# Precedence for VectorE's additions of the projection, and other half steps for its products

## The chip, the cores and the metric

The kernel runs on one core of a Trainium2 chip. The metric is the device time of one execution in microseconds (us). Five engines work side by side, each with an instruction queue of its own: TensorE (PE in the profile) does matrix products and writes them into PSUM; VectorE (DVE) and ScalarE (ACT) read PSUM and do elementwise work; GpSimd (POOL) and SyncE (SP) here only issue transfers between the memories. They wait for each other by semaphores.

## The reference

Sliding-window attention with a distance bias, and after it a gated feed-forward block on 4608 tokens:

```python
q, k, v: (8, 8, 576, 64)                     # batch, heads, sequence, head width
rel = pos[:, None] - pos[None, :]
mask = (rel >= 0) & (rel < 128)
scores = np.where(mask, q @ k.T / sqrt(64) - slope[h] * abs(rel), -1e9)
attn = softmax(scores) @ v                   # (8, 8, 576, 64)
x = attn.transpose(0, 2, 1, 3).reshape(4608, 512)

g = x @ w_gate                               # 512 x 1536
silu = g * (1.0 / (1.0 + np.exp(-g)))
val = x @ w_val                              # 512 x 1536
out = (silu * val) @ w_out                   # 1536 x 512, float32 out
```

The last product, with `w_out`, is called the projection here.

## The kernel before

The 4608 tokens are cut into nine blocks of 512. For each block, the gate and value products fill 12 pairs of PSUM tiles (`pg`, `pv`), one pair for each 128 columns of `w_gate` and `w_val`. Each tile is a group of four matmuls, and is one half step. From a pair, ScalarE makes `tt = tanh(pg / 2)`, VectorE `uu = (tt + 1) * pg` and then `hT = uu * pv`. The factor 0.5 that is missing is applied when the projection leaves PSUM.

```python
    def gate(n, m, pg, c0=0, c1=512):
        ...
        nc.scalar.activation(tt, pg[:, c0:c1], AF.Tanh, scale=0.5)
        nc.vector.scalar_tensor_tensor(out=uu, in0=tt, scalar=one if (n, m) == PIN else 1.0,
                                       in1=pg[:, c0:c1], op0=ALU.add, op1=ALU.mult)

    def val(n, m, pv, c0=0, c1=512):
        ...
        nc.vector.tensor_mul(hT[n][:, m, c0:c1], acted[(n, m)][1][:, c0:c1], pv[:, c0:c1])

    def gate_val(n, m):
        c0 = 384 if (n, m) in acted else 0
        gate(n, m, wide(n, m, "g"), c0)
        yield
        val(n, m, wide(n, m, "v"), c0)
        yield
```

The projection of a block runs during the next block's half steps. It uses a scheme after Strassen and Winograd, with seven products in place of eight, twice for a block (`t` is 0 and 1: two pieces of 128 rows of either row half). Sums of parts of `hT` (`S1` to `S4`, lines 485 to 488, on VectorE) and of `w_out` (`T1` to `T4`) are made ahead. Each product is six matmuls with 256 columns. `X` and `Y` are the two halves of one PSUM buffer, `po`, of which there is one; `p2` is a buffer of the pool that the attention also uses, with four of them. Between two `yield`s lies one step, counted 0 to 6 in what follows:

```python
    def strassen(n, t):
        ...
            po = ps_f.tile([P, 2, HC], FP32, name="po", tag="po", bufs=1)
            X, Y = po[:, 0, :], po[:, 1, :]
            p2 = (ps_f.tile([P, HC], FP32, name="p2", tag="gv") if seeded
                  else ps_a.tile([P, HC], FP32, name="p2", tag="a"))
        ...
        def half_plus(dst, a, b):
            nc.vector.scalar_tensor_tensor(out=dst, in0=a, scalar=factor, in1=b,
                                           op0=ALU.mult, op1=ALU.add)

        product(X, A11, B11, True)              # step 0
        ...
            nc.scalar.mul(p1s, X, factor)
        yield
        product(p2, A12, B21, not seeded)       # step 1
        ...
            half_plus(top[:, 0:HC], p2, p1s)
        ...
        yield
        product(X, S2, T2)                      # step 2
        nc.scalar.mul(u2s, X, factor)
        yield
        product(Y, S1, T1, end)                 # step 3
        ...
            nc.scalar.mul(p5s, Y, factor)
        yield
        product(X, S3, T3)                      # step 4
        half_plus(low[:, HC:DM], X, p5s)
        ...
        yield
        product(Y, S4, B22)                     # step 5
        half_plus(top[:, HC:DM], Y, u2s)
        store(n, t, top, HC if end and t else 0, DM, end)
        yield
        product(X, A22, T4)                     # step 6
        ...
            nc.scalar.mul(low[:, 0:HC], X, factor)
        store(n, t + 2, low, 0, HC if end and t else DM, end)
        yield
```

(The comments with the steps' numbers were added here.) In the loop, a block `n` from 2 to 5 has 24 half steps, `2 * m + half`, and the 14 steps of the projection of block `n - 1` follow those half steps that are in `AT`. After each step the loop lets go of one or two of the sums that wait in `later`:

```python
    AT = {1, 3, 4, 6, 8, 9, 11, 12, 14, 16, 17, 19, 20, 22}

    def ffn():
        for n in range(NBLK):
            if n > 1:
                parts = chain(strassen(n - 1, 0), strassen(n - 1, 1))
            ...
            if n == SEVEN_FROM:                 # 6
                break
            for m in range(NMB):                # 12
                for half, _ in enumerate(gate_val(n, m)):
                    yield 1.0
                    if n > 1 and 2 * m + half in AT:
                        next(parts)
                        yield 0.75
                    if n > 1:
                        for _ in range(1 + (len(later) > 3)):
                            if later:
                                later.pop(0)()
```

The attention is made piece by piece between these steps: scores (`ps`, `psc`) into four PSUM buffers, their exponentials on ScalarE (`ex`, `exc`), the mask on VectorE, the weighted values (`av`), whose division on VectorE gives `rec` and `x`, and the transposed `x` (`px`, `xT`). The blocks 6 to 8 make their gate and value products by seven products as well.

From step 60 on, the order of TensorE alone is that of the program. The other engines' queues are filled by a scheduler, by priority, as it expects the work to become ready; at run time each queue is then worked off in that order:

```python
            if step >= FIXED_FROM and fixed is not None:
                fixed.enter_context(tc.manual_schedule(engines=ENGINES["pe"]))
```

Of the kernel before, what the change touches and what calls it, by code (L numbers as in the profile page):

```python
# [13 lines left out]
ALU = mybir.AluOpType  # L14
# [17 lines left out]
SEVEN_FROM = 6  # L32
# [19 lines left out]
def kernel(  # L52
# [10 lines left out]
    nc = tc.nc  # L63
# [377 lines left out]
    def store(n, j, osb, c0=0, c1=512, two=False):  # L441
        for i, (p0, p1, r0) in enumerate(rows_of(n, j)):
            (nc.scalar if two and i else nc.sync).dma_start(out[r0:r0 + p1 - p0, c0:c1],
                                                            osb[p0:p1, c0:c1])
# [59 lines left out]
    def strassen(n, t):  # L504

        h = hT[n]
        A11, A12 = h[:, 0:HM, 0:256], h[:, HM:NMB, 0:256]
        S1, A22 = h[:, 0:HM, 256:512], h[:, HM:NMB, 256:512]
        S2, S3, S4 = hsum[n]
        cols = slice(t * P, (t + 1) * P)  # L510
        end = n == NBLK - 1
        seeded = SEVEN_FROM <= n + 1 < NBLK
        factor = 1.0 if n >= SEVEN_FROM else 0.5
        if end:
            X, Y = (ps_a.tile([P, HC], FP32, name="po", tag="a", bufs=4) for _ in range(2))
            p2 = ps_f.tile([P, HC], FP32, name="p2", tag="gv")
        else:
# [4 lines that stand above are left out]
        top, low = (opool.tile([P, DM], FP32, name="osb", tag="osb") for _ in range(2))  # L522
        if end and t:
            spare = [opool.tile([P, DM], FP32, name="osb", tag="osb") for _ in range(2)]
            p1s, p5s, u2s = spare[0][:, 0:HC], spare[0][:, HC:DM], spare[1][:, 0:HC]
        else:
            p1s, p5s, u2s = (supool.tile([P, HC], FP32, name=i, tag=i, bufs=1)
                             for i in ("p1s", "p5s", "u2s"))

        def product(dst, a, b, start=False):  # L530
            for m in range(HM):
                nc.tensor.matmul(dst, a[:, m, cols], b[:, m, :], start=(start and m == 0),  # L532
                                 stop=(m == HM - 1), skip_group_check=True)

        def half_plus(dst, a, b):
            nc.vector.scalar_tensor_tensor(out=dst, in0=a, scalar=factor, in1=b,
                                           op0=ALU.mult, op1=ALU.add)

        product(X, A11, B11, True)
        if seeded:  # L540
            nc.scalar.copy(p2, X)
        else:
            nc.scalar.mul(p1s, X, factor)
        yield
        product(p2, A12, B21, not seeded)
        if seeded:
            nc.vector.tensor_scalar_mul(top[:, 0:HC], p2, factor)
        else:
            half_plus(top[:, 0:HC], p2, p1s)
        if end and t:  # L550
            store(n, t, top, 0, HC)
        yield
        product(X, S2, T2)
        nc.scalar.mul(u2s, X, factor)
        yield
        product(Y, S1, T1, end)
        if end and t:
            nc.vector.tensor_scalar_mul(p5s, Y, factor)
        else:
            nc.scalar.mul(p5s, Y, factor)  # L560
        yield
        product(X, S3, T3)
        half_plus(low[:, HC:DM], X, p5s)
        if end and t:
            store(n, t + 2, low, HC, DM, True)
        yield
        product(Y, S4, B22)
# [3 lines that stand above are left out]
        product(X, A22, T4)  # L571
        if end:
            nc.vector.tensor_scalar_mul(low[:, 0:HC], X, factor)
        else:
# [3 lines that stand above are left out]
# [118 lines left out]
                    of[which[0]][name](which[1])  # L696
                yield n, 7 * u + k, name, which

    AT = {1, 3, 4, 6, 8, 9, 11, 12, 14, 16, 17, 19, 20, 22}

    def ffn():

        for n in range(NBLK):
# [8 lines left out]
            for m in range(NMB):  # L712
# [4 lines that stand above are left out]
# [288 lines left out]
```

## Time and profile before

| | before |
|---|---|
| time, median of 3 (lowest, highest) | 345.17 us (344.97, 345.27) |
| span of the profiled execution | 343.0 us |
| TensorE busy | 329.1 us, 96% |
| VectorE busy | 277.5 us, 81% |
| ScalarE busy | 207.6 us, 61% |
| additions of the projection on VectorE (L536) | 42, mostly 417 ns each |

The span is one execution as the profiler saw it. L536 is line 536 of the kernel. A group is named by what it writes and reads, `po<-T,S` for a product that writes `po` from `T` and `S`. Busy matmuls overlap: a matmul of 512 columns is shown with some 379 ns, while the next one starts about 0.21 us after it. The chain that ended last is followed back from the last instruction, at each step to what released it, so its shares say which engine the end hung on. The list of waits sums, for each pair, how long an engine stood still until another released it.

### The profile page before, as it was taken

The numbers are of one execution on the slowest core, as the hardware profiler recorded it, in microseconds if no ns is written. First come the engines' busy times: TensorE is split into PE (matmuls) and PEld (weight loads), VectorE is DVE, ScalarE is ACT, GpSimd is POOL, SyncE is SP. The second block draws the span as 40 slices with busy tenths as digits, with TensorE's granted clock in tenths as the row PEclk, the third lists the DMA queues.
The fourth block names the chain that finished last, engine by engine and source line by source line (L and its number), as shares of the span: only waits on it lengthen the run. The fifth ranks groups of instructions, "written<-read, shape, count | busy, mean of one in ns | idle before, by whom it ended". The sixth has DMA issues, their size and how long they took to land.

```text
span 343.0 us, 7778 instructions
## 1 busy us (share of the span) xinstructions
PE 329.1 (96%) x2983; PEld 218.2 (64%) x2983; DVE 277.5 (81%) x652; ACT 207.6 (61%) x412; POOL 109.6 (32%) x136
## 2 busy tenths in 40 slices
PE   6999989999999999999999999999999999999995
PEld 3484455444456565656565655565788878888884
DVE  6578886999798679988899999999855975775683
ACT  3758676565666755756556547563467666776640
POOL 8968672649674274844017000000000000000000
PEclk9999999999999999999999999999999999999999
DMA  9999999999999999999979912021101101011024
GB/s 153 169 180 176 161 173 149 83 135 163 131 172 140 158 169 169 122 166 136 157 201 135 160 32 78 15 71 39 63 2 61 63 0 64 8 56 63 0 71 116
DMA packets 160037, 37.37 MB, mean 109 GB/s; under 512 B 147328, under 2 KB 155648, under 8 KB 160000
## 3 DMA queue, kind: packets, MB, share of 16 engines
q0 software_dynamic: 118336, 18.62, 84.1%
q1 hardware_dynamic: 40976, 17.64, 28.3%
q10 hardware_dynamic: 688, 0.62, 0.6%
q8 instruction: 23, 0.38, 0.5%
q14 instruction: 14, 0.11, 0.1%
HBM read 37.91 MB, written 9.44 MB: 138 GB/s over the span
## 4 chain that ended last, share of the span: by engine, by line
PE 70%; DVE 19%; ACT 6%; issue 3%; DMA 1%; ACTq 0%; DVEq 0%
PE po L532 15%; PE pg L397 13%; PE pv L397 12%; PE gX L623 8%; PE gY L623 4%; PE av L345 4%; DVE uu L416 3%; DVE hT L427 3%; PE ps L278 3%; PE p L532 2%; PE po L451 2%; PE gZ L623 2%; DVE x L348 2%; ACT ex L284 2%; PE px L371 2%
## 5 line engine op out<-in xcount | busy, mean ns | idle before, releaser
L397 PE MATMUL pv<-xT,wv_sb 128*128 128x512 f16 (+2 forms) x320 | 76.5, 358 | 0.5 <-DVE hT L427 0.2
L397 PE MATMUL pg<-xT,wg_sb 128*128 128x512 f16 (+2 forms) x320 | 75.8, 358 | 0.3 <-DVE xT L373 0.2
L415 ACT ACTIVATE tt<-pg 128x512 f16<-128x512 f32 (+2 forms) x70 | 41.3, 590 | 50.4 <-PE pg L397 49.4
L284 ACT ACTIVATE ex<-ps 128x512 f16<-128x512 f32 x96 | 50.0, 606 | 11.4 <-PE ps L278 11.4
L416 DVE SCALAR_TENSOR_TENSOR uu<-tt,pg 128x512 f16<-128x512 f16 (+2 forms) x69 | 45.8, 664 | 10.5 <-ACT tt L415 10.2
L427 DVE TENSOR_TENSOR hT<-uu,pv 128x512 f16<-128x512 f16 (+2 forms) x70 | 46.5, 665 | 3.6 <-PE pv L397 1.6
L185 POOL DMA_DIRECT2D va<-in_v_dram x40 | 34.2, 862 | 32.8 <-PE av L345 23.9
L397 PEld LDWEIGHTS <-wg_sb 128*128 128x128 f16 x320 | 28.2, 98 | 24.3 <-issue 2.5
L397 PEld LDWEIGHTS <-wv_sb 128*128 128x128 f16 x320 | 28.3, 98 | 24.0 <-issue 2.9
L532 PEld LDWEIGHTS <-hT 128*128 128x128 f16 x384 | 36.8, 98 | 10.4 <-issue 1.1
L191 POOL DMA_DIRECT2D kn<-in_k_dram x39 | 33.3, 858 | 22.0 <-DMA kT<-kn 11.4
L191 POOL DMA_DIRECT2D qn<-in_q_dram x39 | 33.4, 863 | 18.2 <-DMA va<-in_v_dram 11.2
L532 PEld LDWEIGHTS <-S 128*128 128x128 f16 x288 | 27.6, 98 | 10.7 <-issue 2.5
L290 DVE TENSOR_TENSOR ex<-ex,m_reg 128x1024 f16<-128x1024 f16 x42 | 28.6, 685 | 3.2 <-ACT ex L284 3.1
L348 DVE TENSOR_TENSOR x<-av,rec 128x256 f16<-128x256 f32 x72 | 28.5, 418 | 0.4
L532 PE MATMUL po<-T,S 128*128 128x256 f16 x192 | 26.5, 273 | 0.5 <-DVE S L487 0.5
L532 PE MATMUL po<-T,hT 128*128 128x256 f16 x192 | 26.1, 273 | 0.0
L317 ACT ACTIVATE exc<-psc 128x512 f16<-128x512 f32 x40 | 21.3, 608 | 4.1 <-PE psc L313 4.1
L675 DVE TENSOR_TENSOR hT<-s,v 128x512 f16<-128x512 f16 x18 | 7.6, 422 | 18.5 <-ACT s L674 18.5
L345 PEld LDWEIGHTS <-ex 128*128 128x128 f16 x384 | 17.4, 97 | 4.6 <-issue 1.3
L345 PE MATMUL av<-va,ex 128*128 128x65 f16 x384 | 19.3, 193 | 0.7 <-ACT ex L284 0.7
L278 PE MATMUL ps<-qT,kT 64*128 64x256 f16 x192 | 16.6, 272 | 0.4 <-DVE qT L223 0.2
(134 smaller groups left out, 534.9 us busy)
## 6 DMA issues: line engine op xcount, KB each, us to landing
out_dram<-osb SPq DMA_DIRECT2D x32, 256.0 KB, 2.4
va<-in_v_dram POOLq DMA_DIRECT2D x32, 128.0 KB, 8.7
qn<-in_q_dram POOLq DMA_DIRECT2D x31, 128.0 KB, 9.0
kn<-in_k_dram POOLq DMA_DIRECT2D x31, 128.0 KB, 9.5
wg_sb<-in_moe_w_gate_dram POOLq DMA_DIRECT2D x6, 256.0 KB, 7.6
wv_sb<-in_moe_w_val_dram POOLq DMA_DIRECT2D x6, 256.0 KB, 8.2
wo_sb<-in_moe_w_out_dram POOLq DMA_DIRECT2D x2, 768.0 KB, 9.5
kn<-in_k_dram POOLq DMA_DIRECT2D x8, 64.0 KB, 7.3
```

The lines of the kernel that those rows point to most:

```text
L185: nc.gpsimd.dma_start(va[rank][p0:p1, :, 0:D], src)
L191: nc.gpsimd.dma_start(t_[p0:p1], src)
L284: nc.scalar.activation(e[:, o:o + 2, :], banks[q4][par], AF.Exp, scale=scale)
L290: nc.vector.tensor_mul(e[:, o, :], e[:, o, :], reg[:, o, :])
L345: nc.tensor.matmul(av[:, j, :], w, val, start=(n == 0), stop=(n == len(todo) - 1))
L348: nc.vector.tensor_mul(x[:, 4 * half:4 * half + 4, :], av[:, :, 0:D], rec.broadcast_to([P, 4, D]))
L397: nc.tensor.matmul(ps[:, c0:c1], w[:, kb, ms], xT[n][:, kb, c0:c1], start=(kb == 0 and c0 == 0), stop=(kb == NKB - 1 and c1 == 512), skip_ ...
L415: nc.scalar.activation(tt, pg[:, c0:c1], AF.Tanh, scale=0.5)
L416: nc.vector.scalar_tensor_tensor(out=uu, in0=tt, scalar=one if (n, m) == PIN else 1.0, in1=pg[:, c0:c1], op0=ALU.add, op1=ALU.mult)
L427: nc.vector.tensor_mul(hT[n][:, m, c0:c1], acted[(n, m)][1][:, c0:c1], pv[:, c0:c1])
L532: nc.tensor.matmul(dst, a[:, m, cols], b[:, m, :], start=(start and m == 0), stop=(m == HM - 1), skip_group_check=True)
L623: nc.tensor.matmul(dst[:, i, :], w[:, kb, c0 + i * P:c0 + (i + 1) * P], a[:, kb, :], start=(start and i == 0 and kb == 0), stop=(i == 1 an ...
```

## The change

Two things change. `half_plus`, the addition on VectorE after steps 1, 4 and 5, is given high priority in the scheduler for the projections of blocks 1 to 4, which run in the loop's blocks 2 to 5; afterwards it is as before. And the set `AT` is another one, so that some of the 14 steps follow other half steps. The aim is that the additions on VectorE come early in its queue and have two half steps in between, before TensorE needs the buffer `po` again. Nothing of what is computed changes.

```diff
@@ -533,8 +533,9 @@
         def half_plus(dst, a, b):
-            nc.vector.scalar_tensor_tensor(out=dst, in0=a, scalar=factor, in1=b,
-                                           op0=ALU.mult, op1=ALU.add)
+            with tc.high_priority() if n + 1 < SEVEN_FROM else ExitStack():
+                nc.vector.scalar_tensor_tensor(out=dst, in0=a, scalar=factor, in1=b,
+                                               op0=ALU.mult, op1=ALU.add)
@@ -696,7 +697,7 @@
-    AT = {1, 3, 4, 6, 8, 9, 11, 12, 14, 16, 17, 19, 20, 22}
+    AT = {1, 3, 4, 6, 7, 9, 11, 13, 14, 15, 17, 18, 20, 22}
```

In the order of the steps, that is

| step | 0 | 1 | 2 | 3 | 4 | 5 | 6 | 0' | 1' | 2' | 3' | 4' | 5' | 6' |
|---|---|---|---|---|---|---|---|---|---|---|---|---|---|---|
| before | 1 | 3 | 4 | 6 | 8 | 9 | 11 | 12 | 14 | 16 | 17 | 19 | 20 | 22 |
| after | 1 | 3 | 4 | 6 | 7 | 9 | 11 | 13 | 14 | 15 | 17 | 18 | 20 | 22 |

## The prediction

> **What bounds the kernel now.** I first read the page's busy times and the chain that ended last:
>
> ```profile
> PE 329.1 (96%) x2983; PEld 218.2 (64%) x2983; DVE 277.5 (81%) x652; ACT 207.6 (61%) x412; POOL 109.6 (32%) x136
> ...
> PE 70%; DVE 19%; ACT 6%; issue 3%; DMA 1%; ACTq 0%; DVEq 0%
> PE po L532 15%; PE pg L397 13%; PE pv L397 12%; PE gX L623 8%; PE gY L623 4%; PE av L345 4%; DVE uu L416 3%; DVE hT L427 3%; PE ps L278 3%; PE p L532 2%; PE po L451 2%; PE gZ L623 2%; DVE x L348 2%; ACT ex L284 2%; PE px L371 2%
> ```
>
> TensorE (PE) is the bound, and its order is fixed by the program from step 60 on, so the time can shrink only where TensorE stands still. Next, the busy time by stretches of the span. The columns are busy us of PE, weight loads, VectorE (DVE), ScalarE (ACT) and GpSimd. Blocks 2 to 5 of the loop, the ones that change, run from about 97 to 246 us:
>
> ```profile
> 97.00:134.00 37.00, 36.28 (x342) 22.31 (x341) 30.26 (x67) 23.41 (x48) 18.62 (x23) 1.00 1.93 156
> 134.00:171.00 37.00, 36.38 (x349) 22.16 (x347) 33.43 (x80) 22.60 (x47) 16.01 (x19) 1.00 2.01 153
> 171.00:208.00 37.00, 36.16 (x331) 21.81 (x329) 35.83 (x88) 21.65 (x44) 7.59 (x10) 1.00 1.06 124
> 208.00:246.00 38.00, 37.34 (x315) 22.65 (x313) 37.39 (x94) 18.75 (x37) 0.00 (x0) 1.00 0.19 56
> ```
>
> TensorE idles 0.7 to 0.8 us in each stretch; VectorE climbs from 82% to 98% busy. So VectorE runs behind TensorE in the later blocks, and what TensorE needs from it can come late. The waits of TensorE between 97 and 246 us (total us, times, longest) say for what:
>
> ```profile
> PE po L532 <- DVE osb L536: 1.5, 2, 0.8
> PE p L532 <- ACT ex L284: 0.7, 1, 0.7
> PE po L532 <- DVE S L487: 0.5, 1, 0.5
> PE psc L313 <- DVE osb L536: 0.2, 1, 0.2
> ```
>
> The largest is the change's target: a product of the projection (L532) waits for an addition of the projection (L536). The timeline shows one such wait:
>
> ```profile
> 166.82 0.39 PE L371 MATMUL px<-idm,x 128*128 128x128 f16 x4
> ...
> 167.36 0.41 DVE L536 SCALAR_TENSOR_TENSOR osb<-po,p5s 128x256 f32<-128x256 f32 x1
> ...
> 167.83 0.82 PE L532 MATMUL po<-wo_sb,S 128*128 128x256 f16 x6 [0.62 <-DVE osb L536]
> ```
>
> The product waits for `X + p5s` (step 4), yet it is step 5, which writes `Y`. `X` and `Y` are the two halves of the one buffer `po`, so each product in it waits for the evacuation of the product before it, whichever half that used. What matters is therefore how many half steps (a `pg` or a `pv` group of four matmuls) lie between a product and the next one in `po`.
>
> The printed idle is too small, because the matmuls' ends are modelled. By starts, the four transposes at 166.82 come 0.055 us apart, so the product could have started at 167.04 and lost 0.79 us. At 188.62 the same wait costs about 0.9 us, and at 129.13 and 110.24 about 0.2 and 0.1 us that the wait list doesn't show. **Step 5 loses 2.0 us in all.** Counted in the same way, `p` at 119.28 loses 0.85, the wait for `S` near 217.9 loses 0.7 and the wait of `psc` near 218.8 loses 0.3 us.
>
> [...] an addition is late when it stands behind other work, not only when that work feeds it. The trace agrees: at 167.36 it starts 1.24 us after its product's last matmul ends (166.12), behind two `x` and one `hT`. [...] here it took 391 to 425, mostly 417 ns, which I use. [...] A `pg` at 107.07 is followed by the next group at 107.93, 0.86 us for four[...].
>
> **The change, part by part.** No work is added or removed: 5,954 rows on TensorE in both. Four of the fourteen products of a block move, by one half step each (a prime marks the second half, `t = 1`): 4, 4' and 2' come earlier, 0' later.
>
> *Other half steps.* From the two sets AT, half steps between a product and the next in `po`, before to after, first/second half: step 4 to 5 (addition by VectorE) 1/1 to 2/2; step 5 to 6 (VectorE) 2/2 to 2/2; step 3 to 4 (ScalarE, `p5s`) 2/2 to 1/1; step 2 to 3 (ScalarE) 2/1 to 2/2; step 6 to 0' (ScalarE) 1 to 2; step 0 to 2 (ScalarE) 3/4 to 3/2. So the slow evacuator gets the room, and `p5s` pays for it.
>
> What the removed wait needs: TensorE is free about 0.17 us before its last matmul ends (273 ns long, issued 107 ns apart). Free to next start is then 0.17 + lag of the addition + 0.42 + 0.06 handing over (110.18 to 110.24). With the lags of the trace in step 4 (0.56, 0.68, 0.62, 1.24, 1.78, 0.54, 0.62, 0.06 us for the eight halves) that is at most 0.17 + 1.78 + 0.42 + 0.06 = 2.43 us. In the changed order of TensorE the work between 4 and 5 is two half steps and the attention's groups that fall there. For the half with 1.78 it is `pg`, `pv` and `ps`, 0.86 + 0.87 + 0.54 = 2.27 us; for the one with 1.24 (need 1.89) it is `pv`, `pg`, `px`, 1.94 us. The others need at most 1.33 and have 1.7 or more. **So the half steps alone remove 1.8 to 2.0 of the 2.0 us.**
>
> *Precedence.* In the changed order of VectorE the addition of step 4 stands ahead of work that stood before it: of one `uu` in the first half of block 3, of `x`, `x` and `hT` in the second, of `x`, `hT` and `uu` in the first half of block 4; each takes 0.42 to 0.69 us. That shortens just the lags that were left over, so I take the full **-2.0 us**. In block 5 the addition of `p` (step 1) now goes ahead of `x` and `hT`, 0.42 + 0.69 = 1.1 us sooner; it frees the buffer that `psc` waits for: **-0.3 us**, likely. The order also puts one `ex` product (0.69 us) behind the last `S` before step 2 there, which should cut the 0.7 us wait: **-0.35 us** at even odds.
>
> *What it costs.* Step 4 now comes one half step after step 3 and waits for `p5s`, whose duration is
>
> ```profile
> L560 ACT ACTIVATE p5s<-po x15: 383/383/432, 107.0 to 333.7; 128x256 f32<-128x256 f32 x15
> ```
>
> In the eight halves `p5s` ended 1.23, 0.59, 1.09, 1.07, 1.20, 0.70, 0.59 and 0.59 us after TensorE came free, as ScalarE is often still in the four `ex` of the scores. Add 0.06 and compare with the work now between 3 and 4: 0.86 (one half step), 1.40, 1.35, 1.35, 1.11, 1.35, 0.86, 0.86. The first halves of blocks 2 and 4 come short by 0.43 and 0.15: **+0.6 us**. ScalarE's own order changes only by a swap of a `tt` with `p1s` or `u2s`, which moves nothing. The `p` at 119.28 keeps its 0.85: it waits for the first `ex` after a `ps` that stands right before it in both orders.
>
> VectorE, at 97 to 98% in the last two stretches, has to put something back. An `hT` or `uu` delayed by 0.42 us frees its `pg`/`pv` buffer later. The slack there is mostly above 0.9 us, but 0.05 at 186.2 and 0.2 at 173.7. I allow **+0.4 us**.
>
> Sum: -2.0 - 0.3 - 0.35 + 0.6 + 0.4 = about -1.6 us. From 246 us on TensorE is again almost without gaps and nothing else is the bound, so this passes to the end: **345.2 - 1.6 = 343.6 us**.
>
> **The rivals.** (a) *A wait takes the place of the one removed*: `p5s` on ScalarE. For it, the lags of 0.5 to 0.65 us in four of eight halves; against it, ScalarE is only 50 to 60% busy and attention's groups fill most of the shorter gaps. If every half lost 0.4 us, that were 3.2 us and the time 346; at the lags seen it is 0.6. (b) *VectorE as the bound*: additions taken early stand at the head of the queue while their product isn't done, and VectorE idles where it has 2% to spare; then `hT`, `uu` and the sums come late. For it, 37.39 of 38 us busy. Against it, in the trace the lag there is 1 us or more, so the product is done by the time VectorE arrives. It would give 345 to 346. (c) *Only the half steps count*, and the precedence does nothing or hurts a little: about 344. (d) *A transfer hides it*: the loads of attention take the DMA engines up to 171 us. No TensorE wait on DMA shows from 97 us on, so this speaks for nothing.
>
> **Range and chances.** The whole quarrel is about some 4 us of idle TensorE in 150 us. If all goes well (all of the 3.0 us gone, nothing paid), 342.2. If `p5s` and VectorE take back all, 345.2. I set 342.3 to 345.1. Two per cent are 6.9 us, more than all idle time in these blocks together, so faster by that is next to impossible, and slower would need a wait that repeats in every half.
>
> **What would show it.** Right: "po <- osb" gone from TensorE's waits between 97 and 246 us; a short "po <- p5s" at the first half of block 2 in its place; the end of block 5 about 1.6 us sooner; equal busy times on all engines. Wrong: `po <- p5s` in most halves (a); `pv <- uu`, `pg <- hT` or `po <- S` growing to over 1 us (b); a gain before 246 us that isn't there at the end.

## The result and the profile after

| | before | after |
|---|---|---|
| time, median of 4 | 345.13 us | 343.56 us |
| ratio (95% interval) | | 0.9959 (0.9942 to 0.9976) |
| span of the profiled execution | 343.0 us | 341.8 us |
| first product of the projections to first `gX` | 147.87 us | 146.72 us |
| first `gX` to the last matmul | 93.48 us | 93.48 us |

The last two rows are starts of matmuls in the two traces. Inside the changed blocks 1.15 us are saved, and the rest of the kernel keeps all of it. The two profiled executions took 344.81 and 343.57 us, 1.24 us apart. The medians say 1.57 us; their interval (0.8 to 2.0 us) holds all three.

First the busy times of the changed kernel, then its stretches, with the same columns as before:

```profile
PE 329.7 (96%) x2983; PEld 218.6 (64%) x2983; DVE 276.8 (81%) x652; ACT 207.1 (61%) x412; POOL 109.7 (32%) x136
```

```profile
97.00:134.00 37.00, 36.06 (x339) 22.18 (x337) 30.01 (x66) 23.17 (x47) 18.11 (x23) 1.00 1.85 171
134.00:171.00 37.00, 36.69 (x352) 22.43 (x350) 33.61 (x79) 22.93 (x48) 15.73 (x18) 1.00 2.03 164
171.00:208.00 37.00, 36.98 (x332) 21.92 (x330) 36.15 (x89) 21.23 (x44) 7.60 (x10) 1.00 0.94 94
208.00:246.00 38.00, 37.96 (x322) 23.39 (x321) 37.83 (x97) 19.59 (x39) 0.00 (x0) 1.00 0.22 60
```

Every engine has as many instructions as before, and its busy time differs by 0.7 us at most. TensorE idles no longer in the last two stretches (0.02 and 0.04 us), and still does in the first two (0.94 and 0.31 us). The waits of TensorE from 97 to 246 us are now:

```profile
PE p L532 <- ACT ex L284: 0.7, 1, 0.7
PE po L532 <- DVE S L487: 0.3, 1, 0.3
PE po L532 <- ACT p5s L561: 0.3, 1, 0.3
```

`po <- osb` and `psc <- osb` are gone, `p5s` has come in, `p` has stayed. This is step 5 in the first half of block 4, first in the kernel before:

```profile
188.15 0.42 DVE L536 SCALAR_TENSOR_TENSOR osb<-po,p5s 128x256 f32<-128x256 f32 x1
...
188.62 0.81 PE L532 MATMUL po<-wo_sb,S 128*128 128x256 f16 x6 [0.84 <-DVE osb L536]
```

and then in the changed one, where the addition ends 0.8 us before the product starts:

```profile
186.68 0.41 DVE L537 SCALAR_TENSOR_TENSOR osb<-po,p5s 128x256 f32<-128x256 f32 x1
...
187.92 0.83 PE L532 MATMUL po<-wo_sb,S 128*128 128x256 f16 x6
```

The wait for `S` looks like a smaller remainder of the old one, but it isn't: it has another place, the start of block 3, where `p`'s addition now stands ahead of the last third of `S`:

```profile
141.33 0.60 PE L532 MATMUL po<-T,S 128*128 128x256 f16 x4
...
141.44 0.41 DVE L537 SCALAR_TENSOR_TENSOR osb<-p,p1s 128x256 f32<-128x256 f32 x1
...
141.77 0.41 DVE L487 TENSOR_TENSOR S<-hT 128x512 f16<-128x512 f16 x1
...
142.24 0.39 PE L532 MATMUL po<-T,S 128*128 128x256 f16 x2 [0.31 <-DVE S L487]
```

In what follows, waits are counted by starts, as in the prediction. Into and out of a group of scores (`ps`, `psc`) the next start comes about 0.1 us later than elsewhere, in both kernels (before: `pg` at 97.91, `ps` at 98.87, 0.96 us, where a `pg` at 107.07 is followed after 0.86; after: `pv` at 186.42, `ps` at 187.38, 0.96 us); this is usual and not counted.

### The profile page after: what moved, and what is told of

Read it like the earlier page. It is cut to its first block, busy times and chain, and to the rows that moved or that the text cites. A ratio compares the mean times of both kernels' runs of the same rounds, so it can differ in the third digit from the quotient of the medians.

```text
span 341.8 us, 7786 instructions
## 1 busy us (share of the span) xinstructions
PE 329.7 (96%) x2983; PEld 218.6 (64%) x2983; DVE 276.8 (81%) x652; ACT 207.1 (61%) x412; POOL 109.7 (32%) x136
## 4 chain that ended last, share of the span: by engine, by line
PE 74%; DVE 15%; ACT 6%; issue 3%; DMA 1%; ACTq 0%; DVEq 0%
PE po L532 16%; PE pg L397 14%; PE pv L397 14%; PE gX L624 8%; PE av L345 4%; PE gY L624 4%; PE ps L278 3%; PE p L532 2%; DVE hT L427 2%; PE gZ L624 2%; DVE uu L416 2%; ACT ex L284 2%; ACT tt L415 2%; PE po L451 2%; DVE ex L290 2%
```

## Experiments

The kernel before, run beside these on the same chips, took 345.09 to 345.27 us. Ratios are to it. Each edit is shown against the changed kernel unless another run is named. An edit lets the scheduler order VectorE and ScalarE anew everywhere, so what one instruction does is read at its place in the trace.

### The new half steps alone

```diff
-            with tc.high_priority() if n + 1 < SEVEN_FROM else ExitStack():
-                nc.vector.scalar_tensor_tensor(...)
+            nc.vector.scalar_tensor_tensor(...)
     AT = {1, 3, 4, 6, 7, 9, 11, 13, 14, 15, 17, 18, 20, 22}
```

> The new half steps alone, no precedence. Theory A (room between step 4 and step 5 carries the gain, precedence is at most a small extra): no wait of po for an addition longer than 0.2 us, the wait for p5s at the first half of block 2 stays at 0.4 us, the 0.5 us wait for S at the start of block 3 goes (the addition of p no longer stands ahead of that sum), the wait of psc in block 5 comes back with about 0.3 us; time 343.3 to 343.9. Rival B (precedence carries it): time 344.5 or more, with additions that lag by over 1.5 us.

Measured: 344.73 us, ratio 0.9992 (0.9983 to 1.0): at best 0.6 us faster, and perhaps not at all. The time is the one that rival B forecast. Theory A nearly held for step 5, of whose waits 0.2 us is left in block 3 and 0.3 in block 4. But one wait that it put at 0.3 us is the largest of all, for an addition that starts 2.6 us after its product ends. This is the start of block 5 in this run (start, duration, engine):

```profile
216.16 0.89 PE L532 MATMUL po<-T,S 128*128 128x256 f16 x6
216.21 0.39 DVE L487 TENSOR_TENSOR S<-hT 128x512 f16<-128x512 f16 x1
...
216.52 0.42 DVE L348 TENSOR_TENSOR x<-av,rec 128x256 f16<-128x256 f32 x1
...
216.85 0.68 DVE L427 TENSOR_TENSOR hT<-uu,pv 128x512 f16<-128x512 f16 x1
...
217.45 0.68 DVE L290 TENSOR_TENSOR ex<-ex,m_reg 128x1024 f16<-128x1024 f16 x1
218.05 0.41 DVE L536 SCALAR_TENSOR_TENSOR osb<-p,p1s 128x256 f32<-128x256 f32 x1
...
218.52 0.38 PE L313 MATMUL psc<-qT,kT 64*128 64x128 f16 x7 [1.09 <-DVE osb L536]
```

The scores `psc` need the buffer of `p`, whose addition stands behind `x`, `hT` and an `ex` product. By starts it costs 1.25 us. Now the same place in the kernel before:

```profile
215.03 0.68 DVE L290 TENSOR_TENSOR ex<-ex,m_reg 128x1024 f16<-128x1024 f16 x1
...
217.44 0.41 DVE L487 TENSOR_TENSOR S<-hT 128x512 f16<-128x512 f16 x1
...
217.77 0.68 DVE L427 TENSOR_TENSOR hT<-uu,pv 128x512 f16<-128x512 f16 x1
...
217.91 0.39 PE L532 MATMUL po<-T,S 128*128 128x256 f16 x2 [0.51 <-DVE S L487]
...
218.37 0.42 DVE L536 SCALAR_TENSOR_TENSOR osb<-p,p1s 128x256 f32<-128x256 f32 x1
...
218.84 0.38 PE L313 MATMUL psc<-qT,kT 64*128 64x128 f16 x7 [0.15 <-DVE osb L536]
```

There the last third of `S` came first and late, behind an `ex` product, and TensorE had already stood still 0.7 us for it when it asked for `p`'s buffer. The addition cost only 0.3 us more, because another wait ran beside its lateness. In the run with the half steps alone, `S` comes in time (the `ex` product is now behind it), and the addition's lateness shows in full: 1.0 us of waiting became 1.25.

### Precedence alone

```diff
-    AT = {1, 3, 4, 6, 7, 9, 11, 13, 14, 15, 17, 18, 20, 22}
+    AT = {1, 3, 4, 6, 8, 9, 11, 12, 14, 16, 17, 19, 20, 22}
```

> Precedence alone, old half steps. Theory A by its formula (free to next start = 0.17 + lag + 0.42 + 0.06): in the second half of block 3 one hT less (0.69) stands ahead of the addition, so its wait falls from 0.79 to about 0.1; in the first half of block 4 one uu less, so it falls from 0.9 to about 0.25; the two short ones of block 2 stay; no wait for p5s; the wait for S at the start of block 3 appears (0.5), the waits for S and psc in block 5 go (1.0). Sum about -1.3 + 0.5 - 1.0 = -1.8 at best, VectorE standing at the head of its queue takes some of it back: 343.4 to 344.5. If precedence did nothing: 345.1. Rival B: as fast as both parts together, 343.6 or less.

Measured: 344.02 us, ratio 0.9971 (0.9958 to 0.9984), in the middle of theory A's range. The waits of step 5 are 0.2 us in each of blocks 2 and 3 and 0.15 in block 4, about what the formula gave. At the start of block 5 the picture is turned over:

```profile
214.36 0.68 DVE L290 TENSOR_TENSOR ex<-ex,m_reg 128x1024 f16<-128x1024 f16 x1
...
216.44 0.41 DVE L537 SCALAR_TENSOR_TENSOR osb<-p,p1s 128x256 f32<-128x256 f32 x1
...
217.10 0.41 DVE L487 TENSOR_TENSOR S<-hT 128x512 f16<-128x512 f16 x1
...
217.57 0.39 PE L532 MATMUL po<-T,S 128*128 128x256 f16 x2 [0.84 <-DVE S L487]
...
217.90 0.62 PE L313 MATMUL psc<-qT,kT 64*128 64x128 f16 x16
```

The addition goes first and `S` waits behind it: 1.0 us again, where I expected none. Each part alone leaves about 1 us at this place, and only both together remove it, as the changed kernel shows:

```profile
216.19 0.89 PE L532 MATMUL po<-T,S 128*128 128x256 f16 x6
216.23 0.39 DVE L487 TENSOR_TENSOR S<-hT 128x512 f16<-128x512 f16 x1
...
216.54 0.41 DVE L537 SCALAR_TENSOR_TENSOR osb<-p,p1s 128x256 f32<-128x256 f32 x1
...
216.88 0.41 DVE L348 TENSOR_TENSOR x<-av,rec 128x256 f16<-128x256 f32 x1
...
217.01 0.73 PE L313 MATMUL psc<-qT,kT 64*128 64x128 f16 x16
...
217.21 0.67 DVE L427 TENSOR_TENSOR hT<-uu,pv 128x512 f16<-128x512 f16 x1
...
217.81 0.68 DVE L290 TENSOR_TENSOR ex<-ex,m_reg 128x1024 f16<-128x1024 f16 x1
```

`S` and the addition both come before `psc`, and an `x` follows them closely. What stands behind all three is an `hT` and the `ex` product.

### Both parts, precedence only for the additions of po

```diff
-        def half_plus(dst, a, b):
-            with tc.high_priority() if n + 1 < SEVEN_FROM else ExitStack():
+        def half_plus(dst, a, b, ahead=True):
+            with tc.high_priority() if ahead and n + 1 < SEVEN_FROM else ExitStack():
-            half_plus(top[:, 0:HC], p2, p1s)
+            half_plus(top[:, 0:HC], p2, p1s, False)
```

> Both parts, but precedence only for the additions that read po (steps 4 and 5), not for that of p (step 1). Theory A: the precedence of p's addition costs the 0.5 us wait for S at the start of block 3 and saves the 0.3 us wait of psc in block 5; without it the first goes and the second returns: 343.2 to 343.6, the same as or a little faster than the change. If the precedence of p's addition is what brings the gain: 344 or more.

Measured: 344.62 us, ratio 0.9981 (0.997 to 0.9992). This falls on the other side: beside the new half steps (344.73), precedence for the additions of `po`, at which the change aims, brings 0.1 us. The leftovers of step 5 go, and `psc` waits 1.25 us.

### Precedence for p's addition alone

```diff
-        def half_plus(dst, a, b):
-            with tc.high_priority() if n + 1 < SEVEN_FROM else ExitStack():
+        def half_plus(dst, a, b, ahead=False):
+            with tc.high_priority() if ahead and n + 1 < SEVEN_FROM else ExitStack():
-            half_plus(top[:, 0:HC], p2, p1s)
+            half_plus(top[:, 0:HC], p2, p1s, True)
```

> The new half steps with precedence for p's addition (step 1) alone, none for those of po. Theory D (two separate lateness places: step 5 in blocks 2 to 4, which the half steps mostly settle, and the start of block 5, where psc waits 1.25 us for p's addition unless it has precedence): against the half steps alone, the 1.25 us wait of psc goes, the wait for S at the start of block 3 grows from 0.14 to 0.48 us, the leftover waits of step 5 (0.1 and 0.3) stay; 344.73 - 1.25 + 0.34 = 343.8, between 343.5 and 344.1. Rival: the precedence of the additions of po matters as much; then 344.3 or more.

Measured: 343.83 us, ratio 0.9961 (0.9948 to 0.9973), as theory D said, and the interval is nearly that of the whole change. `S` in block 3 waits 0.48 us and step 5 keeps 0.2 and 0.15.

### Precedence for one single instruction

As in the run before, but:

```diff
-            half_plus(top[:, 0:HC], p2, p1s, True)
+            half_plus(top[:, 0:HC], p2, p1s, n == 4 and t == 0)   # all others: no precedence
```

> The new half steps, and precedence for one single instruction: p's addition in the first half of block 5 (the projection n = 4, t = 0), which moves ahead of x, hT and an ex product. Theory D (the precedence is worth what that one place is worth): the 1.25 us wait of psc goes, all else stays as with the half steps alone (p5s 0.42, step 5 0.1 and 0.3, S in block 3 0.14): 344.73 - 1.2 = 343.5, as fast as the whole change. Rival: precedence works by all its twenty-four additions together; then 344.3 or more.

Measured: 343.93 us, ratio 0.9964 (0.9952 to 0.9977). The time lies between theory and rival, 0.4 us off either, but the ratio can't be told from that of the whole change, and from the first product to the first `gX` the trace has 146.77 us, after 147.55 with the half steps alone and 146.72 with the whole change. The 1.25 us wait is gone; the other waits are there as expected, and two more, at steps 6 of block 5: 0.17 and 0.21 us. The changed kernel has these two as well. There they show as starts that come later than the group before allows:

```profile
226.46 1.03 PE L397 MATMUL pv<-xT,wv_sb 128*128 128x512 f16 x4
...
227.02 0.41 DVE L537 SCALAR_TENSOR_TENSOR osb<-po,u2s 128x256 f32<-128x256 f32 x1
...
227.49 0.70 PE L532 MATMUL po<-T,hT 128*128 128x256 f16 x5
```

The `pv` group takes 0.86 us, so `po` could have started at 227.32; the addition of step 5 ended at 227.43. Neither of the two shows in the runs where `psc` waits 1.25 us. So with TensorE that much ahead, VectorE seems to fall behind it later in the block and to take back 0.4; no run tests this by itself.

### The last S ahead, with the old half steps

Precedence for all additions as in the run with precedence alone, and for the last third of the sum `S2`:

```diff
+        def second():
+            with tc.high_priority() if ahead else ExitStack():
+                nc.vector.tensor_sub(s2, a21, a11)
-                lambda: nc.vector.tensor_sub(s2, a21, a11),
+                second,
...
+        # in sums(n, c): ahead = c == 2 and n + 1 < SEVEN_FROM
...
-    AT = {1, 3, 4, 6, 7, 9, 11, 13, 14, 15, 17, 18, 20, 22}
+    AT = {1, 3, 4, 6, 8, 9, 11, 12, 14, 16, 17, 19, 20, 22}
```

> Precedence for the additions with the old half steps (344.02), and precedence for the last third of the sum S2 too, which then stands ahead of the reciprocals, two x and p's addition at the start of block 5. Theory D: the 1.0 us wait for S at the start of block 5 is one of order on VectorE, not of its load, and goes, the one in block 3 (0.24) falls: 342.9 to 343.3. Rival C (VectorE is so full there that the wait only moves, to psc, pv or an addition): 343.8 to 344.1.

Measured: 343.91 us, ratio 0.9959 (0.9946 to 0.9971). This is rival C's outcome: the time is that of precedence alone (344.02). The wait in block 3 is gone, and the one at the start of block 5 has moved for the third time:

```profile
214.26 0.68 DVE L290 TENSOR_TENSOR ex<-ex,m_reg 128x1024 f16<-128x1024 f16 x1
...
215.80 0.42 DVE L487 TENSOR_TENSOR S<-hT 128x512 f16<-128x512 f16 x1
...
216.03 0.82 PE L536 MATMUL po<-T,S 128*128 128x256 f16 x6
...
216.96 0.66 DVE L427 TENSOR_TENSOR hT<-uu,pv 128x512 f16<-128x512 f16 x1
...
217.53 0.42 DVE L348 TENSOR_TENSOR x<-av,rec 128x256 f16<-128x256 f32 x1
...
218.00 0.40 PE L313 MATMUL psc<-qT,kT 64*128 64x128 f16 x7 [0.77 <-DVE x L348]
```

(The edit moves the lines behind it by four; L536 is the products' line here.) Now `S` and `p` are in time, and `psc` waits 0.94 us for the buffer whose values the second `x` reads. So TensorE needs three things from VectorE at this place, in this order: the last `S`, `p`'s addition and the second `x`. The kernel before, the half steps alone and this run each have an `ex` product and an `hT` ahead of the last of the three. Precedence alone has the `ex` ahead, and `S`, which is needed first, behind the other two. The changed kernel has the three in the order of need, and `hT` and `ex` behind them; there the second `x` is over by 217.29, and the second half of `psc` starts 0.06 us later. What removes the wait here is not to bring one thing forward but to put behind it what nobody needs yet.

### Step 3 a half step earlier

```diff
-    AT = {1, 3, 4, 6, 7, 9, 11, 13, 14, 15, 17, 18, 20, 22}
+    AT = {1, 3, 4, 5, 7, 9, 11, 13, 14, 15, 16, 18, 20, 22}
```

> The change with step 3 a half step earlier in both halves, so that two half steps lie between it and step 4, and one between step 2 and step 3. Theory A: the 0.42 us wait for p5s at the first half of block 2 goes, u2s (whose lag is 0.04 us) needs 0.66 us of the 0.86 it has and costs nothing: about 343.1. Rival C (VectorE is the bound in blocks 3 to 5, so what is won in front of it is lost to it): 343.5, with larger waits for S, pv or additions.

Measured: 343.29 us, ratio 0.9952 (0.9938 to 0.9965). This lies between theory A and rival C. The wait for `p5s` is gone from the trace and `u2s` costs nothing. From the first product to the first `gX` the trace has 146.30 us, 0.42 less than the changed kernel; 0.27 show in the median, which the intervals can't tell from 0.42 or from nothing. Smaller waits change both ways: `ps` in block 4 waits 0.34 in place of 0.19 us for an `x`, a `psc` in block 3 0.13 in place of none, and the last step 6 of block 5 none in place of 0.2.

### p's addition without precedence in block 3

Against the run with step 3 earlier (`half_plus` takes `ahead` as in the run with precedence only for the additions of `po`):

```diff
-            half_plus(top[:, 0:HC], p2, p1s)
+            half_plus(top[:, 0:HC], p2, p1s, n != 2)
```

> As the run with step 3 a half step earlier (343.29), but p's addition has no precedence in block 3 (the projection n = 2), where it stood ahead of the last S. Theory: the 0.48 us wait for S falls to 0.14 and nothing takes its place: 342.95. Rival C (VectorE gives it back later): 343.3.

Measured: 343.22 us, ratio 0.994 (0.9928 to 0.9953). The wait for `S` falls from 0.48 to 0.15 us as expected, so precedence had made it. The median hardly moves; between theory (342.95) and rival (343.3) it decides nothing by itself. The stretch from the first product to the first `gX` is 146.21 after 146.30 us; 0.11 us of the difference is a new wait of a `ps` in block 3, and the rest stays open.

### p one half step later in block 2

Against the run before:

```diff
+    AT_2 = {1, 3, 4, 5, 7, 9, 11, 13, 15, 16, 17, 18, 20, 22}
-                    if n > 1 and 2 * m + half in AT:
+                    if n > 1 and 2 * m + half in (AT_2 if n == 2 else AT):
```

> As the run before it in this list, and in block 2 the second half's steps 1, 2 and 3 follow half steps 15, 16 and 17 in place of 14, 15 and 16, so that a pv group of 0.86 us lies between the scores and p, which had waited 0.85 us for the first exponential of those scores. Theory: that wait goes, as there is now one half step in which the exponential ends; p5s has one half step plus the scores and costs nothing: 342.1 to 342.3. Rival: the four exponentials delay p5s or the next evacuation, 342.6 to 343.

Measured: 342.47 us, ratio 0.9923 (0.9909 to 0.9936): 0.75 us less in the median, and as much in the trace (145.46 after 146.21 from the first product to the first `gX`). The time lies between theory and rival, because 0.1 of the 0.85 us is the usual gap behind scores, which `pv` now has in place of `p`. The cause was the one named: `p` had stood right behind the scores whose first exponential frees its buffer.

```profile
117.93 0.61 PE L278 MATMUL ps<-qT,kT 64*128 64x256 f16 x8
...
118.47 1.04 PE L397 MATMUL pv<-xT,wv_sb 128*128 128x512 f16 x4
118.59 2.06 ACT L284 ACTIVATE ex<-ps 128x512 f16<-128x512 f32 x4
...
119.34 0.82 PE L532 MATMUL p<-wo_sb,hT 128*128 128x256 f16 x6
```

The `pv` group now fills that time, and `p` starts without a wait.

### Precedence for p's addition in block 5 only

Against the run before:

```diff
-            half_plus(top[:, 0:HC], p2, p1s, n != 2)
+            half_plus(top[:, 0:HC], p2, p1s, n == 4)
```

> As the run with p later in block 2 (342.47), but p's addition has precedence only in block 5, not in blocks 2 and 4 either. In block 4 it stood ahead of an x that ps waits for (0.35 us in place of the usual 0.1). Theory D: that wait goes and nothing takes its place: 342.2. Rival C: 342.5, with another wait grown.

Measured: 342.31 us, ratio 0.9918 (0.9905 to 0.9932), against 342.47; the wait of `ps` in block 4 is gone as expected and a `pv` soon after it waits 0.12 us, as rival C had it in part; 0.16 us is within the spread of the runs. Between 97 and 247 us the list of TensorE's waits is empty, and the last stretch shows it:

```profile
208.00:246.00 38.00, 37.99 (x324) 23.65 (x323) 37.10 (x93) 19.72 (x40) 0.00 (x0) 1.00 0.24 56
```

VectorE is nearly as busy as before and TensorE doesn't idle. By starts, some 0.7 us in five places of more than 0.1 us remain. This version is faster than the kernel before by 0.8%, and its interval lies wholly below that of the changed kernel (0.9942 to 0.9976), whose median is 1.25 us higher.

## Why the prediction was right in time, and where its steps were wrong

The time (343.6 predicted, 343.56 measured) and the direction held; that the median falls within 0.04 us is luck, as the trace saves 1.15 us where the prediction had 1.6. The terms, by starts in the trace of the changed kernel:

| term | predicted | found |
|---|---|---|
| step 5 waits for an addition | -2.0 | -2.0 |
| wait of `psc`, start of block 5 | -0.3 | -0.3 |
| wait for `S`, start of block 5 | -0.35 | -0.6 |
| `p5s` | +0.6 | +0.4 |
| given back by VectorE | +0.4 | +1.1 |
| sum | -1.6 | -1.3 |

"Found" for the last row is `S` in block 3 (0.48), steps 6 (0.44, three places), `pv` and `ps` in block 4 (about 0.2). The sum is taken before rounding; all starts that come over 0.05 us late add up to 3.80 us before and 2.53 after. The stretch got shorter by 1.15 us, which leaves 0.1 for places smaller than that. So the total is near partly because two terms erred in opposite directions.

- **Step 5.** Confirmed as a whole. The half steps alone left 0.5 of the 2.0 us, where I had put 0 to 0.2; precedence alone left 0.5; both together nothing. Here either part does most of the work.
- **"So the half steps alone remove 1.8 to 2.0."** Of these waits they removed 1.5, but of the time 0.36 us by the medians, at most 0.6, and 0.32 of the stretch. This is the step that failed: I treated the waits as separate terms. The waits for `S` and of `psc` at the start of block 5 were one lateness of VectorE, seen at two places; with the first gone, the second grew to 1.25 us.
- **Precedence.** "I take the full -2.0" gave it a small part, and 0.3 for the addition of `p`. Removing it from `p` alone cost 1.06 us (344.62 against 343.56), and giving it to one single addition, after the new half steps, brought 0.8 (344.73 to 343.93). Beside the new half steps, what it brings lies in block 5, not at `po`.
- **`p5s`.** Block 2: 0.43 predicted, 0.42 found. Block 4: 0.15 predicted, none found in the changed kernel, 0.1 in three of the runs.
- **`p` at 119.28.** Kept its 0.85 us (0.75 without the usual gap), for the reason given.
- **Given back.** The sign was right, the size wrong by more than half. I looked at the slack of the `pg` and `pv` buffers, where only 0.1 us was lost. I did not look at `S`, although the changed order has `p`'s addition ahead of the last `S` in block 3.
- **"Almost without gaps" from 246 us on.** This was misread. The stretch that follows in the kernel before leaves TensorE idle for 0.6 us, nearly as much as in the stretches that change:

```profile
246.00:283.00 37.00, 36.40 (x333) 32.27 (x331) 25.50 (x58) 25.79 (x51) 0.00 (x0) 1.00 0.09 33
```

It did no harm, as the part from the first `gX` on took 93.48 us in both kernels. "5,954 rows on TensorE" stands in no trace; the pages list 2983 matmuls and as many weight loads in both.

Of the rivals, (a) is refuted as more than one half: `p5s` cost one wait. (c) is refuted: the half steps alone brought 0.36 us, and precedence beside them 1.2. (b) said that VectorE would stand still at an addition whose product isn't done. In the trace of the changed kernel VectorE is idle before none of the 24 additions with precedence, so that did not happen; what (b) said would follow, late sums, came in part: at the start of block 3 the last third of `S` starts 0.33 us after the addition in front of it (141.44 to 141.77), and its wait is 0.48 us; without the addition's precedence in block 3 it was 0.15. This takes back a good third of what is won, not all. Of (d) nothing shows: no wait of TensorE on a transfer is listed between 97 and 247 us in any of the runs. That here the order of the queue and not the load decides is shown by the last version, with VectorE busy for 276.7 us, after 276.8 in the changed kernel, and no wait listed. Not tried was an `X` and a `Y` in buffers of their own, beside the eight PSUM buffers that the kernel has. That the shared buffer makes step 5 wait rests on the traces: in either kernel no product in `po` between 97 and 246 us starts before the evacuation of the product before it has ended, and in the kernel before four of the eight steps 5 start 0.05 to 0.06 us after that end, though the evacuation read the other half. No run here shows whether the chip needs this wait or the program merely sets its semaphores by whole buffers.

## What to carry to other kernels

Here two engines were both nearly full (from 208 to 246 us before the change, TensorE 37.34 and VectorE 37.39 of 38 us), and the waits in the trace were not terms that could be added: one wait hid the lateness of the next (with the 0.7 us for `S` gone, `psc` waited 1.25 us in place of 0.3), and moving an addition forward in VectorE's queue did not help where it passed what was needed sooner (precedence alone: 1.0 us for `S`). So list, for the place, everything the waiting engine needs from the other within the next few microseconds, and ask which of the queue's items none of them is. And test precedence on the one instruction that stands at a wait, before giving it to a whole class: here, beside the new half steps, one addition of twenty-four did nearly all the good (0.78 of 0.83 us of the stretch), and those of `p` in blocks 3 and 4 did harm (0.3 and 0.2 us of waits).

## What the runs showed of the hardware that was not expected

Nothing new about a single instruction. Unexpected was how steadily about the same lateness reappeared at the start of block 5: 1.0 us (before, `S` and `psc`), 1.25 (half steps alone, `psc` on the addition), 1.0 (precedence alone, `S`), 0.94 (with `S` ahead, `psc` on `x`), and 0.1 in the changed kernel, while VectorE was busy for 276.7 to 277.5 us of the span in all five.
